# Routed attention with a squared-ReLU feed-forward: how the second pair of heads is turned, and how the first one is marked

## The chip, the cores and the metric

The kernel runs on one core of a Trainium2 chip. Its engines are TensorE (PE; its weight loads are PEld), VectorE (DVE), ScalarE (ACT), GpSimd (POOL) and SyncE (SP, which here only issues transfers). The metric is the device time of one execution in microseconds: 864.44 us before, the median of three runs (864.1 to 864.48).

## The reference

```python
# attention: q, k, v are (4, 8, 768, 64), centroids (8, 16, 64)
q_assign = np.argmax(np.einsum('bhsd,hcd->bhsc', q_n, c_n), axis=-1)   # normalised rows
k_assign = np.argmax(np.einsum('bhsd,hcd->bhsc', k_n, c_n), axis=-1)
mask = q_assign[:, :, :, None] == k_assign[:, :, None, :]
scores = np.where(mask, scale * np.matmul(q, k.transpose(0, 1, 3, 2)), -1000000000.0)
attn = softmax(scores)                     # over the keys
x = (attn @ v), brought to (3072, 512)
# feed-forward: w_in (512, 2048), w_out (2048, 512)
out = np.maximum(x @ w_in, 0.0) ** 2 @ w_out
```

A query thus attends to the keys of its own head that have the same nearest centroid.

## The kernel before

**Work.** The 32 heads are taken two at a time: 16 pairs, numbered from 0. One pass of the loop `for p in range(NG)` is the stage of pair p. A pair's q and k (768 rows of 64, two heads side by side in 128 partitions) are needed turned, with the 64 numbers of a row along the partitions: `qkT[p]`, 12 blocks of 128 columns, six of q and six of k. The scores are made in nine tiles, each two heads wide and 1024 columns in PSUM: tiles 0 to 5 hold a block of 128 keys against 512 queries, tiles 6 to 8 two blocks of keys against the other 256. For each tile TensorE runs `mask` (L456) and `score` (L447), ScalarE the exponential (L463) and VectorE the sums (L466). Then `times_v` (L481) multiplies all exponentials by v, `evict` (L490) copies the result, `add_up` (L500), `invert`, `spread` and `finish` divide by the sums. Three PSUM buffers (`ps_sc`, taken by `begin`) go round among the tiles, the logits and the add-up; two more banks, `V` and `M`, take the products with v. Beside the stages the weights of the feed-forward are loaded in blocks and rounded for later; after the last stage the feed-forward itself runs on TensorE to the end.

**Turning.** Pair 0 is turned on TensorE by multiplying with the identity (`turn_first`, L280). Pair 1 also (`turn`, L295: three calls of 16 matrix instructions each, copied to `qkT[1]` by ScalarE). From pair 2 on it is done by transfers: `split_words` (L315, L316) copies q or k on ScalarE into a tile `flat`, low and high halves of the 4-byte words apart, and writes it to DRAM as `words`; `turn_words` (L327) reads `words` back by one transposing transfer of 2-byte elements. `flat` has its place among the six buffers of q and k.

**Marks.** `logits` (L335) multiplies the turned rows by the normalised centroids; `turn_logits` (L346) brings the 16 logits of a row side by side; `number` finds the largest. Its steps are a maximum, a comparison `is_ge`, a product with 16, 15, ..., 1, a maximum again (so of equal maxima the first counts), and then for pair 0 an `is_equal` that gives a one-hot tile `oh`. `turn_onehot` turns it on TensorE (L402), and ScalarE and VectorE copy it out so that one matmul adds 0 where the clusters agree and a large negative number where not. For the other pairs `number` makes three rows of the number and its square (`marks`), which go to DRAM (`far`, L383) and back into `rows` (two transfers, L386) and do the same as three rows in place of sixteen.

**Order.** Each engine's instructions run in the order in which the program writes them, SyncE's transfers too. An instruction that waits holds up all behind it on its engine; a transfer issued from SyncE or ScalarE that must wait holds up that engine's queue. What SyncE issues in the first stages, in this order: q and k of pairs 0, 1, 2 and v of pair 0; then, at the top of stage 0,

```python
if p == 0:
    load_qk(3)
    load_ahead(0)          # weight blocks 0, 1, 2
...
load_v(p + 1)
```

and later in stage 0 `far` and `rows` of pair 1, `turn_words(2)`, the words of pair 3; in stage 1 `far_r` (`invert`, L515), `turn_words(3)`, two transfers of `spread` (L522), v of pair 2, `far` and `rows` of pair 2 (made by `number(2)` behind tile 3), the words of pair 4. `load_ahead(n)` loads weight blocks until n + 3 have been loaded. A block is rounded at the end of the stage of its number (`round_1`, ScalarE). In the later stages p the marks of pair p + 1 are made at the top of the stage.

At the end the sums' reciprocals, kept in `seen`, are examined: where one is not usable, a slower path computes all again (`check_sums`, L1707).

## Time and profile before

| | |
|---|---|
| median of three runs | 864.44 us |
| profiled execution | 866.05 us, its span 864.3 us |
| granted TensorE clock, mean | 0.999 |
| TensorE busy | 854.1 us, 99% of the span |
| VectorE / ScalarE / GpSimd busy | 86% / 52% / 28% |
| DMA | 174.36 MB, 202 GB/s in the mean |
| stage 0, from pair 0's logits to its first product with v | 10.35 to 27.00 us |
| stage 1, first mask to first product with v | 35.67 to 46.37 us |
| stage 2, first mask | 55.70 us |

A row of the timeline has start, length (both us), engine, line, operation, what is written from what, shape and count; idle time of the engine ahead of it and what ended it stand in brackets. SPq and ACTq are the issues of transfers: their length is that of the issue, not of the transfer. Ends of matmuls are modelled, so TensorE's waits show less as idle time than as later starts.

### The profile page before, as it was taken

The page shows a single profiled execution, that of the slowest core. Times are in us where ns is not written, and L with a number is a line of the kernel's source. Part 1 is how long each engine was busy: PE and PEld are TensorE (multiplying, and loading weights), DVE is VectorE, ACT ScalarE, POOL GpSimd, SP SyncE. Part 2 cuts the span into 40 slices and gives each one's busy share as a digit, 9 for nine tenths or more (in the row PEclk, how much of TensorE's full clock was granted, in tenths as well). Part 3 has the DMA queues.
Part 4 walks back from the last instruction along what each step waited for, and adds up shares of the span by engine and source line. Part 5 has one row for each costly group of instructions (what it writes and reads, how often), then busy time and mean ns, then how long its engine had stood idle before and what let it go on. Part 6 is the DMA issues. An engine that isn't in the chain of part 4 may idle for free.

```text
span 864.3 us, 15572 instructions
## 1 busy us (share of the span) xinstructions
PE 854.1 (99%) x5883; PEld 648.7 (75%) x5883; DVE 739.8 (86%) x1192; ACT 452.7 (52%) x697; POOL 245.9 (28%) x232
## 2 busy tenths in 40 slices
PE   9999999999999999999999999999999999999997
PEld 6444444444444445557899899999999999999997
DVE  5799888888888899899778888789888998888786
ACT  4877766677776557753212593122259322594120
POOL 0000001000000046772496537040233902337000
PEclk9999999999999999999999999999999999999999
DMA  7686797777766217829897634549447895444542
GB/s 257 152 202 177 208 283 197 191 195 189 192 173 162 83 45 246 255 76 323 328 334 267 233 135 143 211 136 338 173 174 235 285 372 200 170 146 135 222 151 74
DMA packets 149732, 174.36 MB, mean 202 GB/s; under 512 B 57258, under 2 KB 126994, under 8 KB 146322
## 3 DMA queue, kind: packets, MB, share of 16 engines
q1 hardware_dynamic: 133090, 152.94, 56.1%
q10 hardware_dynamic: 16560, 20.35, 7.2%
q8 instruction: 48, 0.79, 0.4%
q14 instruction: 34, 0.28, 0.1%
HBM read 111.98 MB, written 50.27 MB: 188 GB/s over the span
## 4 chain that ended last, share of the span: by engine, by line
PE 95%; DVE 2%; DMA 2%; ACT 0%; issue 0%; DVEq 0%
PE bank L1383 24%; PE bank L1111 16%; PE sc L447 14%; PE av_a L481 10%; PE bank L811 8%; PE bank L1280 6%; PE more L1111 5%; PE av_b L481 5%; PE sc L456 4%; PE sc L335 1%; PE sc L500 1%; DMA wt<-w_far 1%; DVE home L557 1%; DMA q_raw<-in_q_dram 0%; PE sc L280 0%; PE av_a L295 0%
## 5 line engine op out<-in xcount | busy, mean ns | idle before, releaser
L463 ACT ACTIVATE ex<-sc 128x1024 f32<-128x1024 f32 x144 | 144.4, 1026 | 37.5 <-PE sc L447 31.6
L447 PE MATMUL sc<-qkT 64*128 64x512 f32 (+1 forms) x768 | 150.5, 484 | 0.0
L167 POOL TENSOR_TENSOR w_in<-w_in,w_raw 128x512 int32<-128x512 int32 x16 | 21.4, 1340 | 296.4 <-DVE w_in L159 296.4
L1096 POOL TENSOR_TENSOR g<-g,home 128x384 f32<-128x384 f32 x60 | 61.0, 1048 | 156.0 <-DVE home L1195 101.7
L447 PEld LDWEIGHTS sc<-qkT 64*128 64x128 f32 x768 | 65.6, 188 | 42.1 <-issue 30.2
L481 PE MATMUL av_a<-ex,v_raw 128*64 128x512 f32 x384 | 85.9, 596 | 0.0
L466 DVE TENSOR_TENSOR total<-total,ex 128x1024 f32<-128x1024 f32 x64 | 78.7, 1229 | 6.5
L1640 ACT COPY spare<-bank 128x128 f32<-128x128 f32 x35 | 9.2, 263 | 133.2 <-issue 69.7
L1383 PE MATMUL bank<-wt,l 128*128 128x128 f32 x544 | 72.0, 275 | 0.2 <-DVE l L557 0.2
L1383 PE MATMUL bank<-wt,home 128*128 128x128 f32 x552 | 70.5, 275 | 0.0
L1383 PEld LDWEIGHTS bank<-wt,l 128*128 128x128 f32 x544 | 66.2, 192 | 0.4 <-DVE l L557 0.4
L1383 PEld LDWEIGHTS bank<-wt,home 128*128 128x128 f32 x552 | 66.0, 192 | 0.0
L1195 DVE TENSOR_TENSOR g<-bank,g 128x384 f32<-128x384 f32 (+2 forms) x108 | 53.2, 504 | 13.4 <-PE bank L1111 9.6
L481 PEld LDWEIGHTS av_a<-ex,v_raw 128*64 128x64 f32 x384 | 26.1, 137 | 51.0 <-issue 50.0
L1078 ACT COPY home<-bank 128x384 f32<-128x384 f32 x66 | 30.9, 480 | 58.2 <-PE bank L1111 56.8
L456 PE MATMUL sc<-rows 64*128 64x512 bf16 (+1 forms) x360 | 58.8, 323 | 0.0
L787 ACT ACTIVATE g<-g 128x768 f32<-128x768 f32 (+1 forms) x77 | 55.8, 725 | 2.4
L786 ACT ACTIVATE g<-g 128x768 f32<-128x768 f32 (+1 forms) x77 | 54.9, 713 | 2.9 <-DVE g L1195 1.5
L481 PE MATMUL av_b<-ex,v_raw 128*64 128x256 f32 x384 | 44.2, 379 | 0.0
L481 PEld LDWEIGHTS av_b<-ex,v_raw 128*64 128x64 f32 x384 | 27.6, 137 | 20.7 <-issue 5.7
L456 PEld LDWEIGHTS <-rows 64*128 64x128 bf16 x360 | 17.5, 94 | 33.6 <-issue 30.4
L1383 PE MATMUL bank<-wt,g 128*128 128x128 f32 x304 | 38.8, 275 | 0.0
(296 smaller groups left out, 1855.4 us busy)
## 6 DMA issues: line engine op xcount, KB each, us to landing
wt<-right_far SPq DMA_DIRECT2D x11, 1792.0 KB
wt<-w_far SPq DMA_DIRECT2D x20, 896.0 KB
words<-flat SPq DMA_DIRECT2D x26, 384.0 KB
w_raw<-in_moe_w_in_dram SPq DMA_DIRECT2D x16, 512.0 KB
w_raw<-in_moe_w_out_dram SPq DMA_DIRECT2D x16, 512.0 KB
wt<-right_far SPq DMA_DIRECT2D x7, 1024.0 KB
v_raw<-in_v_dram SPq DMA_DIRECT2D x16, 384.0 KB
raw<-raw_far SPq DMA_DIRECT2D x12, 512.0 KB
```

The lines of the kernel that those rows point to most:

```text
L447: nc.tensor.matmul(sc[i][:, e, cols], lhsT=qkT[pair][rows, NCH + c], rhs=qkT[pair][rows, n.start // P : n.stop // P], start=first, stop=no ...
L456: nc.tensor.matmul(sc[i][:, e, cols], lhsT=ohT[pair][rows, 1, c * P : (c + 1) * P], rhs=ohT[pair][rows, 0, columns(i)], start=first, stop= ...
L463: nc.scalar.activation(out=ex[i], in_=sc.pop(i), func=ACT.Exp, scale=SCALE)
L466: eng.tensor_tensor(out=out, in0=a, in1=b, op=ALU.add)
L481: nc.tensor.matmul(bank[D * e : D * (e + 1), 0 : n.stop - n.start], lhsT=raw_v[pair][:, e, c], rhs=ex[i][:, e, cols], start=c == 0, stop=c ...
L786: nc.scalar.activation(out=to, in_=to, func=ACT.Relu)
L787: nc.scalar.square(to, to)
L811: nc.tensor.matmul(bank, lhsT=operands[j][0][:, kk], rhs=operands[j][1][:, kk], start=(kk == 0), stop=(kk == H2 - 1),)
L1096: nc.gpsimd.tensor_tensor(out=of_four(to, s)[:, f, half], in0=of_four(base, s)[:, f, half], in1=beside[s][:, u], op=ALU.add,)
L1111: nc.tensor.matmul(bank[:, QT * u : QT * (u + 1)], lhsT=lefts[j, s](u)[i], rhs=operand[i], start=begins and u == 0, stop=True, skip_group_ ...
L1195: nc.vector.tensor_tensor(out=out, in0=one, in1=two, op=ALU.add)
L1383: nc.tensor.matmul(bank, lhsT=left[:, f], rhs=rhs[:, f], start=(f == 0), stop=(f == F4 - 1))
```

## The change

Pair 1 is now turned as the later pairs are. Behind pair 0's marks ScalarE splits its words (`split_words(1, i, nc.scalar)`), with `flat` in a buffer of the exponentials; SyncE issues `turn_words(1)` first in stage 0, in two transfers, q and k apart, each when its words have landed. `turn` and its copies go. `logits(1)` moves from behind tile 2 to ahead of tile 8 and writes to bank `M`; the last sum of tiles 0 to 5 comes behind pair 1's marks. `turn_words(2)` moves behind them too, and so does the load of pair 1's v. Of the weight blocks only block 0 is loaded in stage 0 (`load_ahead(-2)`); blocks 1 and 2 come in stage 1 by `load_ahead(0)`, behind v of pair 2. Pair 3's words keep their place.

Pair 0's one-hot tile is written by the `is_ge` itself, so that equal maxima give more than one mark. `count_marks` counts them: where a partition's marks are not 24 in number, the new last column of `seen` is not usable, and the slower path runs. The last quarter of pair 0's turned rows is copied by ScalarE and VectorE, half each (`by_two`). In stage 1 the scores of tiles 0 and 1 are made ahead of their masks.

```diff
--- before.py
+++ after.py
@@ -221,7 +221,7 @@
             scalar2=of_query, op0=ALU.mult, op1=ALU.add,
         )
 
-    seen = const.tile([P, NG * NBL], F32, name="seen")
+    seen = const.tile([P, NG * NBL + 1], F32, name="seen")
 
     oh = accp.tile([P, NBL, 2, D], BF16, name="oh", tag="part")
     nc.vector.memset(oh, 0.0)
@@ -286,22 +286,6 @@
         if which == 1 and i == 1:
             raw.pop(0)
 
-    def turn(pair, part, bank):
-        if part == 0:
-            qkT[pair] = qktp.tile([P, 2 * NCH, P], F32, name="qkT")
-        for i in range(4):
-            which, c = divmod(4 * part + i, NCH)
-            for e in range(2):
-                nc.tensor.matmul(
-                    bank[D * e : D * (e + 1), P * i : P * (i + 1)],
-                    lhsT=raw[pair][which][:, e, c], rhs=ident, start=True, stop=True,
-                )
-        nc.scalar.copy(
-            out=qkT[pair][:, 4 * part : 4 * part + 4].rearrange("p c n -> p (c n)"), in_=bank
-        )
-        if part == 2:
-            raw.pop(pair)
-
     words = {}
 
     def split_words(pair, which, queue=nc.sync):
@@ -309,7 +293,13 @@
             return
         if which == 0:
             words[pair] = dram.tile([2 * NCH, P, 2, 2 * D], U16, name="words")
-        flat = loads.tile([P, NCH, 2, 2 * D], U16, name="flat", tag="qk")
+        if pair == 1:
+            spare = expp.tile([P, 2, 512], F32, name="ex").bitcast(U16)
+            flat = spare.rearrange("p a n -> p (a n)")[:, 0 : 4 * S // 2].rearrange(
+                "p (c two d) -> p c two d", c=NCH, two=2
+            )
+        else:
+            flat = loads.tile([P, NCH, 2, 2 * D], U16, name="flat", tag="qk")
         src = raw[pair][which].bitcast(U16).rearrange("p h c (d two) -> p h c two d", two=2)
         for e in range(2):
             nc.scalar.copy(out=flat[:, :, :, D * e : D * (e + 1)], in_=src[:, e])
@@ -324,10 +314,13 @@
         if pair >= NG:
             return
         qkT[pair] = qktp.tile([P, 2 * NCH, P], F32, name="qkT")
-        nc.sync.dma_start(
-            qkT[pair].rearrange("p c n -> p (c n)").bitcast(U16),
-            words.pop(pair).rearrange("c p two d -> (c p two) d"), transpose=True,
-        )
+        far = words.pop(pair)
+        for i in range(0, 2 * NCH, NCH if pair == 1 else 2 * NCH):
+            c = slice(i, i + (NCH if pair == 1 else 2 * NCH))
+            nc.sync.dma_start(
+                qkT[pair][:, c].rearrange("p c n -> p (c n)").bitcast(U16),
+                far[c].rearrange("c p two d -> (c p two) d"), transpose=True,
+            )
 
     def logits(pair, bank):
         hp = pair % HP
@@ -355,17 +348,17 @@
             return t.unsqueeze(2).to_broadcast([P, n, C])
 
         nc.vector.reduce_max(out=mx, in_=src, axis=AX.X)
+        if pair == 0:
+            nc.vector.tensor_tensor(
+                out=oh.rearrange("p b e c -> p (b e) c")[:, :, 0:C], in0=src, in1=over_c(mx),
+                op=ALU.is_ge,
+            )
+            return
         nc.vector.tensor_tensor(out=best, in0=src, in1=over_c(mx), op=ALU.is_ge)
         nc.vector.tensor_tensor(
             out=best, in0=best, in1=order.unsqueeze(1).to_broadcast([P, n, C]), op=ALU.mult
         )
         nc.vector.reduce_max(out=mx, in_=best, axis=AX.X)
-        if pair == 0:
-            nc.vector.tensor_tensor(
-                out=oh.rearrange("p b e c -> p (b e) c")[:, :, 0:C], in0=best, in1=over_c(mx),
-                op=ALU.is_equal,
-            )
-            return
         squared = small.tile([P, n], F32, name="squared")
         nc.vector.tensor_tensor(out=squared, in0=mx, in1=mx, op=ALU.mult)
         for i, of in enumerate((squared, mx, squared)):
@@ -388,13 +381,23 @@
                 far[:, :, NBL * e : NBL * (e + 1)].rearrange("f g b i -> f g (b i)"),
             )
 
+    def count_marks():
+        marked = small.tile([P, 1], F32, name="marked")
+        nc.vector.reduce_sum(
+            out=marked, in_=oh.rearrange("p b e c -> p (b e) c")[:, :, 0:C], axis=AX.XY
+        )
+        nc.vector.tensor_scalar(
+            out=seen[:, NG * NBL :], in0=marked, scalar1=2.0 * NBL, scalar2=0.5,
+            op0=ALU.is_equal, op1=ALU.mult,
+        )
+
     def turn_onehot():
         spare = expp.tile([P, 2, 512], F32, name="ex").bitcast(BF16)
         ohT[0] = spare.rearrange("p a n -> p (a n)")[:, 0 : 2 * S].rearrange(
             "p (a n) -> p a n", a=2
         )
 
-        for half, bank in enumerate((sc.pop("oh")[:, 0], M)):
+        for half, bank in enumerate((V, M)):
             n = NBL // 2
             blocks = slice(n * half, n * (half + 1))
             po = bank.bitcast(BF16)[:, 0 : n * P].rearrange("p (b g i) -> p b g i", b=n, g=4)
@@ -606,18 +609,25 @@
             load_weights(loaded)
             loaded += 1
 
+    def by_two(out, in_):
+        nc.scalar.copy(out=out[:, 0:QT], in_=in_[:, 0:QT])
+        nc.vector.tensor_copy(out=out[:, QT:], in_=in_[:, QT:])
+
+    QT = TB // 2
     centroids_norm()
     turn_first(0, 0, V, nc.scalar.copy)
     turn_first(0, 1, M, nc.scalar.copy)
     halves = [ps_sc.tile([P, 2, 512], F32, name="sc")[:, 0] for _ in range(2)]
     turn_first(1, 0, halves[0], nc.scalar.copy)
     centroids_turned()
-    turn_first(1, 1, halves[1], nc.vector.tensor_copy)
+    turn_first(1, 1, halves[1], by_two)
     logits(0, begin("ls"))
-    for i in ("oh", 0, 1):
+    for i in range(2):
         begin(i)
     turn_logits(0)
     number(0)
+    for i in range(2):
+        split_words(1, i, nc.scalar)
 
     first_sums = []
     x_early, w_early = x_sums(FEED[0]), []
@@ -629,8 +639,9 @@
 
     for p in range(NG):
         if p == 0:
+            turn_words(1)
             load_qk(3)
-            load_ahead(0)
+            load_ahead(-2)
         if p == HP + 1:
             nc.sync.dma_start(x_far[FEED[3]], xT.pop(FEED[3]))
         if p:
@@ -642,25 +653,31 @@
         if 2 < p + 1 < NG:
             turn_logits(p + 1)
             number(p + 1)
-        load_v(p + 1)
         if p:
+            load_v(p + 1)
             load_ahead(p - 1)
 
 
         if p == 0:
             for i in range(2):
-                turn(1, i, (V, M)[i])
                 score(p, i, 0, True)
             turn_onehot()
+            count_marks()
             for t in rows_of:
                 nc.vector.memset(t, 0.0)
-            turn(1, 2, V)
+            begin(2)
+            score(p, 2, 0, True)
             for i in range(NB):
-                if i == 2:
-                    begin(i)
-                    score(p, i, 0, True)
                 mask(p, i, 0, False)
                 exponential(i)
+        elif p == 1:
+            for i in range(2):
+                begin(i)
+                score(p, i, 0, True)
+            for i in range(2):
+                mask(p, i, 0, False)
+                exponential(i)
+            tile_of(p, 2)
         else:
             for i in range(NB):
                 tile_of(p, i)
@@ -669,7 +686,6 @@
         add(nc.vector, first, ex[0], ex[1])
         if p == 1:
             tile_of(p, NB)
-        if p < 2:
             logits(p + 1, begin("ls"))
             turn_logits(p + 1)
             number(p + 1)
@@ -677,17 +693,25 @@
         for i in range(NB, NCH):
             if p != 1 or i > NB:
                 tile_of(p, i)
-            add(nc.vector, first, first, ex[i])
+            if p or i + 1 < NCH:
+                add(nc.vector, first, first, ex[i])
         if p == 0:
             for i in range(2):
                 split_words(2, i, nc.scalar)
-            turn_words(2)
         else:
             split_words(p + 3, 0)
 
 
         for i in range(NCH, NCH + NB):
             tile_of(p, i)
+            if p == 0 and i == NCH + 1:
+                sc["ls"] = M.rearrange("p (a n) -> p a n", a=1)
+                logits(1, sc["ls"])
+                turn_logits(1)
+                number(1)
+                turn_words(2)
+                load_v(1)
+                add(nc.vector, first, first, ex[NCH - 1])
         part = accp.tile([P, 2, 512], F32, name="part")
         add(nc.vector, part, ex[NCH], ex[NCH + 1])
         add(nc.vector, part, part, ex[NCH + 2])
@@ -1704,7 +1728,7 @@
         every = more.tile([1, 1], F32, name="every", tag="more")
         nc.tensor.matmul(every, lhsT=fine, rhs=ups[:, 0:1], start=True, stop=True)
         nc.vector.tensor_scalar(
-            out=flag[0:1], in0=every, scalar1=UP * float(P * NG * NBL), scalar2=None, op0=ALU.is_lt
+            out=flag[0:1], in0=every, scalar1=UP * float(P * (NG * NBL + 1)), scalar2=None, op0=ALU.is_lt
         )
 
     class Rounding:
```

## Rows read from the trace of the kernel before

**Rows 1.** The page's chain that ended last, shares of the span by engine.
```profile
PE 95%; DVE 2%; DMA 2%; ACT 0%; issue 0%; DVEq 0%
```

**Rows 2.** Timeline of TensorE in the stages of pairs 0 to 2.
```profile
19.50 0.85 PE L335 MATMUL sc<-qkT,cnT 128*32 128x384 f32 x8
...
27.00 5.37 PE L481 MATMUL av_a<-ex,v_raw 128*64 128x512 f32 x24
...
35.67 0.39 PE L456 MATMUL sc<-rows 64*128 64x512 bf16 x2
...
46.37 5.37 PE L481 MATMUL av_a<-ex,v_raw 128*64 128x512 f32 x24
...
55.70 0.39 PE L456 MATMUL sc<-rows 64*128 64x512 bf16 x2
```

**Rows 3.** Chain of waits, 10 to 28 us: start, length, what.
```profile
11.92 1.02 PE av_a L295 x16
12.94 1.06 PE sc L447 x4
...
16.86 1.05 PE av_a L295 x16
```

**Rows 4.** Timeline of VectorE, 10 to 22 us.
```profile
10.47 0.56 DVE L285 COPY qkT<-sc 128x384 f32<-128x384 f32 x1 [0.92 <-PE sc L280]
...
13.16 0.56 DVE L358 TENSOR_TENSOR best<-lt,mx 128x384 bf16<-128x384 f32 x1
...
14.94 0.56 DVE L364 TENSOR_TENSOR oh<-best,mx 128x384 bf16<-128x384 bf16 x1
...
21.54 0.57 DVE L346 STREAM_TRANSPOSE lt<-sc 128x384 f32<-128x384 f32 x1
```

**Rows 5.** Timeline of ScalarE, 16 to 30 us.
```profile
16.56 0.87 ACT L410 ACTIVATE ex<-sc 128x384 bf16<-128x384 bf16 x2 [0.90 <-PE sc L402]
...
18.42 2.86 ACT L463 ACTIVATE ex<-sc 128x1024 f32<-128x1024 f32 x3
...
24.77 1.55 ACT L315 COPY flat<-q_raw 128x768 uint16<-128x768 uint16 x2
...
28.88 1.03 ACT L463 ACTIVATE ex<-sc 128x1024 f32<-128x1024 f32 x1 [0.46 <-ACT flat L315]
```

**Rows 6.** Timeline of SyncE: issues of transfers.
```profile
10.88 1.41 SPq L128 DMA_DIRECT2D w_raw<-in_moe_w_in_dram  x3
...
25.76 0.38 SPq L383 DMA_DIRECT2D far<-marks_t  x1
28.60 1.68 SPq L386 DMA_DIRECT2D rows<-far  x2
31.34 5.14 SPq L327 DMA_TRANSPOSE qkT<-words  x1
...
41.60 3.71 SPq L327 DMA_TRANSPOSE qkT<-words  x1
...
46.64 1.55 SPq L105 DMA_DIRECT2D v_raw<-in_v_dram  x1
48.28 0.42 SPq L383 DMA_DIRECT2D far<-marks_t  x1
51.36 1.52 SPq L386 DMA_DIRECT2D rows<-far  x2
...
77.07 3.25 SPq L327 DMA_TRANSPOSE qkT<-words  x1
```

**Rows 7.** DMA rate in 40 slices: 10:21, 31:42, 41:52 and 76:87 us.
```profile
GB/s 380 374 369 240 89 128 168 279 397 406 402 268 223 253 209 149 179 238 253 343 283 358 358 402 343 432 402 361 380 378 309 207 194 115 91 54 39 28 22 11
...
GB/s 84 112 357 419 296 73 101 221 139 174 172 111 151 182 195 323 323 276 189 176 304 238 10 7 37 290 289 290 315 348 350 344 343 350 346 350 259 0 0 0
...
GB/s 136 0 0 0 0 0 23 216 183 27 122 106 182 165 269 285 292 289 292 288 250 61 190 279 346 268 134 56 78 128 212 352 374 315 145 166 195 296 374 313
...
GB/s 22 20 28 2 0 0 0 0 56 243 85 59 171 289 291 289 290 290 290 290 239 90 268 302 302 235 231 99 24 2 0 5 0 0 0 0 145 190 290 363
```

## The prediction

> **What bounds the kernel now.** I read the page first, then the chain of waits over the first 28 us, then the timelines of VectorE, ScalarE, TensorE and SyncE's queue, and last the DMA rate in fine slices. TensorE is busy for 99% of the span (the table above) and is 95% of the chain that ended last [rows 1]: time is won only by taking work or waits out of TensorE's order, and whatever makes TensorE wait costs its full length. Everything that the change touches lies in the stages of pairs 0 and 1 (before 56 us). From the stage of pair 2 on the order is the old one, so I reduce the question to one event: when does the first mask matmul of pair 2 start? Before it is at 55.70 [rows 2]; I add its shift to the time. The sum is made against the profiled execution (866.05 us, span 864.3), which is 1.61 above the median 864.44; a forecast for the median is the sum less 1.61.
>
> **Turning pair 1 on TensorE (removed).** Three batches of 16 instructions stand in the chain at 1.02 to 1.05 us each, from the one at 11.92 to the one at 16.86 [rows 3]: 3.09 us. A score behind a turn costs 1.06 there; behind a score I take 0.86, an estimate: the 1.09 of a tile (below) less 0.23 for its mask. So 0.2 comes back once.
>
> **First marks by the maxima alone.** Of VectorE's steps after the logits, the `is_ge` at 13.16 now writes the one-hot tile, and three steps up to the one at 14.94 go [rows 4], 0.56 each with gaps: one-hot ready at 13.5 in place of 15.5. This is needed, not gained: without the turns TensorE has only two scores (1.06 + 0.86) between the logits and the one-hot transposes and would otherwise wait. The count (a reduction like the 0.56 one, and a small step) stands behind the one-hot copies on VectorE, ahead of two memsets and of the first sum, which waits for exponentials: nothing. The extra column of `seen`: nothing. Copying the last turned half on two engines halves the 0.56 us copy at 10.47 [rows 4], for which the logits wait: it is over at 10.83 in place of 11.03, and the logits, whose end at 11.92 is where the first turn starts in the chain [rows 3], end at 11.72: 0.2 gained.
>
> **Splitting pair 1 on ScalarE (added).** The same four copies and two DMA issues for pair 2 take from 24.77 to the next exponential at 28.88: 4.11 us [rows 5]. Pair 1's q and k were long there (TensorE turned them from 11.85 without a wait), so the copies start at 10.85, behind ScalarE's half of the turned tile, and hold ScalarE till 14.96; the one-hot copies behind them (0.87, [rows 5]) end at 15.85. TensorE gets there by 11.72 (logits) + 1.92 (two scores) + 0.77 (one-hot: what is left to 16.86 of the chain behind two turns and two scores from 11.92) + 1.06 (third score) = 15.47, so it waits 0.4. The exponentials then run from about 16.5 and not 18.42 [rows 5], and they set the pace: three score buffers, so tile 3 waits for exponential 0 (17.5), where TensorE has been done at 16.6: 0.9 lost. A tile takes 1.09: pair 1's nine tiles and one group of logits (0.85) lie between 35.67 and 46.37 [rows 2]. Six tiles from 17.5 and pair 1's logits, now ahead of tile 8, bring the products with v to 24.8 or 24.9, against 27.00 [rows 2]: 2.2 gained of the 3.3 removed.
>
> **Pair 1's transposing transfers.** The key words are issued at 14.5, 0.4 before ScalarE is free again. Pair 2's went out as long before the exponential at 28.88 [rows 5] and let SyncE's queue go on at 31.34 [rows 6], so 2.9 later: landed at 17.4. A transposing transfer of a whole pair on a quiet queue (issued at 77.07) has its traffic over by 81.8 [rows 6, 7]; half of one some 3.5 us: 20.9. Bounds: 2 us, and the 7.4 that pair 2's took beside other loads [rows 6, 7]. The logits of pair 1 come at 22.9 (one tile and their own 0.85 ahead of 24.8): I take no wait. Queued behind on SyncE are pair 3's loads and one weight load; both were used behind the exponentials at 28.88, and are there in time by 5 us and more.
>
> **Pair 1's marks.** VectorE began to read pair 1's logits at 21.54 [rows 4], and `far`, the marks' way out, went at 25.76 [rows 6]: 4.22 us. It begins now at 23.75, so `far` goes at 28.0, and by the 2.84 from `far` to the row transfers and their 1.68 [rows 6] these are issued by 32.5. Pair 1's tiles now begin with two bare scores: the products and the add-up took 8.67 us before (27.00 to 35.67, [rows 2]), so the scores start at 33.5 and the first mask at 35.4. That is behind the rows' landing by any of the bounds below, so no wait. I take 0.2 us for the changed order and 0.3 for waits on exponentials, which start later in the stage: pair 1's products begin at 33.5 + 10.7 + 0.5 = 44.7 against 46.37 [rows 2], and 9.33 later (46.37 to 55.70) pair 2's first mask would come by TensorE's own order, at 54.0: 1.7 us gained.
>
> **What SyncE's queue makes of it.** It runs in written order. Pair 2's transposing transfer was issued at 31.34, now at 32.5 behind the later rows; v of pair 1 now follows it (0.39 MB, 1.1 us at the 350 GB/s of [rows 7]). Before, pair 3's words ran undisturbed for 2.5 us (38.7 to 41.2, [rows 7]) and the next transposing transfer was released at 41.60 [rows 6]. In place of a transfer that ran 7.4 us beside a load from ScalarE's queue (that load is now over before) I take the quiet 4.7: 32.5 + 4.7 + 1.1 + 2.5 + 0.4 = 41.2. So far even.
>
> But behind it, ahead of pair 2's `far`, now stand two weight loads that the old kernel had issued with a third at 10.88 [rows 6]: `load_ahead(-2)` leaves them to the stage of pair 1. Before, v at 46.64 and `far` at 48.28 follow each other; v's traffic ends at about 50.4, and the rows can be issued at 51.36, when `far` has landed [rows 6, 7]. `far` landed only after v's traffic, as if it stood behind it. Two loads of 0.524 MB each cost 2.8 us at the 370 GB/s that [rows 7] reach and 4.1 at 255, the mean over the forty slices of the stretch in which such loads ran before. I take 3.2, nearer the low end, since the old loads ended in a tail that nothing followed. Then: v over at 50.0, weights at 53.2, `far` landed (0.95 later, as before) at 54.15, the rows' two issues 1.5 (1.52 in [rows 6]) and their landing 1.0 (bounds: 0.7, a small transfer with no delay, and 2.8, the latest that leaves no wait at 55.70): the mask at 56.65. TensorE, there at 54.0, waits 2.65. **Sum: 56.65 - 55.70 = +0.95 us, 867.0 for the profiled execution, 865.4 for the median.**
>
> The Trainium skill, *DMA: Bandwidth & Descriptors*, section "Queues, rings and completion order", says that on each DMA engine a queue's descriptors are taken in ring order. By that rule `far` can't pass the weight loads, and the forecast stands; were small transfers let through, the time would be that of the first rival below. The trace agrees: `far`, issued at 48.28, landed some 0.95 us after v's traffic ended and not before it.
>
> **Rivals.** (1) *Not late.* `far` passes the weights, or these fill gaps in the traffic (61 and 56 GB/s slices stand in [rows 7]), and pair 2's mask starts at 54.0 or at best 53.0, if the waits on ScalarE cost less: -1.7 to -2.7, 861.7 to 862.7. For it: the old stretch from 41 to 52 us has many slices under 200 GB/s [rows 7], so there is room; against: that room lies mostly ahead of the transposing transfer's traffic, where the weights are not yet issued. (2) *Slower: pair 2's transposing transfer is starved again.* Place: the queue from 32.5. Price: 7.4 in place of 4.7, and all behind it is 2.7 later: +3.65, 868.1. It decides once the transfer takes over about 5.5 us, from which the sum is beyond +1.73. For it: the old transfer in this place ran with breaks, down to 10 and 7 GB/s [rows 7]; against: the load that it shared the engines with has moved away. (3) *Slower: pair 1's turned halves come after 22.9*, since the first transposing transfer of the old kernel was its slowest (5.14 us of issue, 3.25 at 77.07 [rows 6]). At 7.4 for the second half it lands at 24.8 + 0.4: 2.3 us of wait, which `far`, rows and queue all inherit: +3.2, 867.7.
>
> **How the numbers follow.** Forecast (late by the weights): 0.62, from +0.3 (weights 2.8, rows' landing 0.7, queue 0.3 the earlier for it) to +2.8 (weights 4.1, landing 2.0), 864.7 to 867.2. Not late: 0.15. Starved: 0.14. Pair 1 late: 0.09. A measurement of this kernel tells about 0.2% (1.73 us) from no change, so same is 862.7 to 866.2. Faster is 0.13, all of the first rival but its edge; same is 0.02 from there, 0.48 of the forecast and 0.03 of mild forms of the others, 0.53; slower is the forecast's upper end, 0.14, with 0.20 of the two slow rivals: 0.34. The range takes half of each side: 862.4 to 867.8.
>
> **What would show it.** Right: no L295 turns and the products with v of pair 0 starting at 24 to 25.5; a wait of TensorE of 2 to 3.5 us ahead of pair 2's first mask (L456 `rows`), and on SyncE a wait of 4 us or more between pair 2's `far` and its rows, with two `w_raw` issues ahead of them; from there to the end the old span within 0.3 us. Wrong: no wait there (rival 1), a logits wait for a transposing transfer near 23 us (rival 3) or near 38 (rival 2), or a gain or loss that arises after 60 us, for which I see no cause.

## The result, and the profile after

The changed kernel takes 871.92 us in the median (16 runs, 867.05 to 879.19) against 864.11 for the kernel before in the same session (16 runs, 861.78 to 866.38): ratio 1.0106, interval [1.0086, 1.0127]. It is slower, and above the range of the forecast. The profiled execution takes 872.58 us (span 870.7), 6.5 more than the one before. Medians and ratios leave out executions that took far longer than all others of their kernel (one of e15 below, at 2294.76 us, and three of the kernel before).

The executions of the changed kernel differ by 12.1 us, those of the kernel before by 4.6. The mean granted clock goes with it: 0.997 in the fastest of the changed kernel, 0.989 in the slowest. The profiled one has 0.995 and 8.4 us at half the clock; the slowest must have some 19 (an estimate: 2.2 times the shortfall), at places that no trace shows. What follows is the account of one execution, near the median.

TensorE after, timeline of the stages of pairs 0 to 2, to be read against [rows 2]:

```profile
20.53 0.85 PE L328 MATMUL av_b<-qkT,cnT 128*32 128x384 f32 x8
...
22.50 5.37 PE L484 MATMUL av_a<-ex,v_raw 128*64 128x512 f32 x24
...
33.00 0.81 PE L459 MATMUL sc<-rows 64*128 64x512 bf16 x6
...
37.60 0.85 PE L328 MATMUL sc<-qkT,cnT 128*32 128x384 f32 x8 [1.86 <-DMA qkT<-words]
...
55.97 0.39 PE L459 MATMUL sc<-rows 64*128 64x512 bf16 x1 [2.69 <-DMA rows<-far]
56.74 0.61 PE L459 MATMUL sc<-rows 64*128 64x512 bf16 x1 [0.38 <-DMA rows<-far]
56.75 2.31 PE L450 MATMUL sc<-qkT 64*128 64x512 f32 x4
```

The products with v of pair 0 start 4.5 us earlier, pair 2's logits (before at 40.08) 2.5 earlier, behind a wait for the transposing transfer, and pair 2's first masks 0.3 and 1.0 later, behind a wait for the row transfers. SyncE's issues, the answer to [rows 6]:

```profile
25.68 0.37 SPq L376 DMA_DIRECT2D far<-marks_t  x1
27.35 1.67 SPq L379 DMA_DIRECT2D rows<-far  x2
29.14 4.91 SPq L320 DMA_TRANSPOSE qkT<-words  x1
...
40.85 2.69 SPq L320 DMA_TRANSPOSE qkT<-words  x1
...
44.89 0.54 SPq L105 DMA_DIRECT2D v_raw<-in_v_dram  x1
45.48 0.94 SPq L128 DMA_DIRECT2D w_raw<-in_moe_w_in_dram  x2
46.47 0.43 SPq L376 DMA_DIRECT2D far<-marks_t  x1
53.71 1.52 SPq L379 DMA_DIRECT2D rows<-far  x2
```

`far` goes 1.8 us earlier than before and its rows 2.35 later: 7.2 us between them in place of 3.1, with two weight loads ahead of `far`. What follows is in the table by stretches (from:to, length, then busy time and instructions of PE, PEld, DVE, ACT, POOL, granted clock, DMA share, GB/s), of the kernel after:

```profile
56.70:60.10 3.40, 3.35 (x10) 2.18 (x12) 2.01 (x7) 1.00 (x1) 0.00 (x0) 0.50 0.67 200
...
606.30:609.70 3.40, 3.40 (x13) 3.40 (x12) 0.00 (x0) 1.16 (x3) 0.00 (x0) 0.50 0.98 324
```

and of the kernel before:

```profile
56.70:60.10 3.40, 3.40 (x22) 1.50 (x20) 3.22 (x7) 3.00 (x3) 1.22 (x1) 1.00 0.32 67
...
606.30:609.70 3.40, 3.40 (x23) 3.40 (x22) 1.95 (x5) 0.96 (x2) 0.00 (x0) 1.00 0.90 296
```

Twice TensorE stood still and then got the lower level (0.50, 1.2 GHz) for 3.4 us: in the same 3.4 us it did 10 matmuls in place of 22, and 13 in place of 23. Its largest waits after (line, tile, releaser: sum, times, longest):

```profile
PE sc L459 <- DMA rows<-far: 3.1, 2, 2.7
PE bank L1135 <- DMA raw<-raw_far: 2.3, 1, 2.3
PE sc L328 <- DMA qkT<-words: 1.9, 1, 1.9
...
PE bank L1135 <- DVE spare L560: 0.7, 1, 0.7
```

Aligning the two traces matmul by matmul, the kernel after is 2.5 us ahead at pair 2's logits, 1.0 behind at pair 2's second mask, 2.7 behind at 60 us (the half clock), 1.25 at 507 us, and 6.4 behind from 610 us to the end. (The fall of about a microsecond near 492 us belongs to the trace of before: e4 below, the old kernel with a wider tile, gains 0.9 there too.) So there are two losses: one in stages 1 and 2, foretold, with a half clock behind it that wasn't; and one of 5.2 us near 600 us, in the feed-forward part, whose order of instructions the change leaves alone.

The second in rows. ScalarE's and SyncE's issues near 587 us before:

```profile
584.96 2.23 ACTq L1591 DMA_DIRECT2D out_dram<-g  x4
...
587.32 0.81 SPq L968 DMA_DIRECT2D wt<-w_far  x2
588.35 1.18 SPq L1771 DMA_DIRECT2D xT<-x_far  x2
592.16 0.32 SPq L937 DMA_DIRECT2D raw<-raw_far  x1
```

and after:

```profile
586.19 2.88 ACTq L1615 DMA_DIRECT2D out_dram<-g  x4
...
586.71 0.81 SPq L992 DMA_DIRECT2D wt<-w_far  x2
589.53 7.56 SPq L1795 DMA_DIRECT2D xT<-x_far  x2
598.16 0.32 SPq L961 DMA_DIRECT2D raw<-raw_far  x1
```

Before, the two weight loads go when all four stores `out_dram<-g` are issued; after, they go between the first store and the last, the second `xT` load waits 6.9 us for a store, and `raw` is issued 6.0 us later. What the DMA view has of instruction loads (queue 8), before in 583:584 us, and after in 587:588, is one each:

```profile
q8 instruction: 1, 0.02, 5.5%
```

These are loads of 16,384 bytes, 48 over the span; they are TensorE's code: with 160 recorded TensorE instructions more (e6 below) there are 49, and the places of the loads move with the count. The page counts 5883 matmul records and as many weight loads before, 5835 of each after: the removed turns are 96 recorded instructions, so each code load falls at another place of the same work.

### The profile page after: what moved, and what is told of

It reads as the page before. It is cut to its first block, busy times and chain, and to the rows that moved or that the text cites. A ratio compares the mean times of both kernels' runs of the same rounds, so it can differ in the third digit from the quotient of the medians.

```text
span 870.7 us, 15481 instructions
## 1 busy us (share of the span) xinstructions
PE 853.2 (98%) x5835; PEld 649.2 (75%) x5835; DVE 740.4 (85%) x1191; ACT 453.2 (52%) x699; POOL 245.6 (28%) x232
## 3 DMA queue, kind: packets, MB, share of 16 engines
q1 hardware_dynamic: 136226, 153.73, 56.6%
## 4 chain that ended last, share of the span: by engine, by line
PE 87%; DVE 8%; DMA 3%; issue 1%; ACT 0%; SPq 0%; DVEq 0%; ACTq 0%
PE bank L1407 22%; PE bank L1135 16%; PE sc L450 14%; PE av_a L484 9%; PE bank L835 8%; PE more L1135 5%; PE av_b L484 4%; PE bank L1304 4%; PE sc L459 3%; PE sc L328 1%; DMA far<-marks_t 1%; PE sc L503 1%; DMA qkT<-words 1%; DVE spare L1219 1%; DVE x_t L560 1%
## 5 line engine op out<-in xcount | busy, mean ns | idle before, releaser
L450 PE MATMUL sc<-qkT 64*128 64x512 f32 (+1 forms) x768 | 152.5, 488 | 0.0
L450 PEld LDWEIGHTS sc<-qkT 64*128 64x128 f32 x768 | 67.8, 189 | 41.9 <-issue 30.8
L459 PE MATMUL sc<-rows 64*128 64x512 bf16 (+1 forms) x360 | 60.8, 325 | 3.1 <-DMA rows<-far 3.1
```

The source lines that it names most:

```text
L450: nc.tensor.matmul(sc[i][:, e, cols], lhsT=qkT[pair][rows, NCH + c], rhs=qkT[pair][rows, n.start // P : n.stop // P], start=first, stop=no ...
L459: nc.tensor.matmul(sc[i][:, e, cols], lhsT=ohT[pair][rows, 1, c * P : (c + 1) * P], rhs=ohT[pair][rows, 0, columns(i)], start=first, stop= ...
```

## The experiments

Each was timed in five rounds beside the kernel before. "Shift" is how much later than in the profile of before the same matmul starts. The upper clock begins at 3.9 us (e8) to 10.0 (before), as it happens, and that alone moves what follows: pair 0's products start at 22.50 in after, at 24.38 in e15, where it begins 3.4 us later. So shifts of two traces compare only to about 2 us, while a step within one trace is sharper.

**Where weight blocks 1 and 2 stand (e1, e2, e3) and the tile layout (e4).** e1 is the kernel after, with the loads back in stage 0:

```diff
-            load_ahead(-2)
+            load_ahead(0)
```

> The changed kernel with weight blocks 1 and 2 loaded in stage 0 again, behind pair 3's q and k. Queue theory (the two weight loads ahead of pair 2's `far` make TensorE wait about 3 us before pair 2's first mask, and the halved clock that follows costs 1.7 more): the mask comes at 53 to 54 us in place of 56.7, the clock stays at its upper level from the ramp to the end, and the time falls by 4 to 9 us to 861 to 867. Layout theory (the extra column of `seen` moves the buffers allocated behind it and slows transfers near 600 us): it stays at 868 to 873, with the wait for `raw` near 604 us. Turning theory (the transposing transfers of pair 1 themselves cost it, by the 1.9 us wait of pair 2's logits): the wait at 36 to 38 us stays, the time falls by 1 to 2 us at most.

870.63 us, 1.0070 [1.0042, 1.0097]. In stage 0 the three loads delay pair 1's `far` and rows (rows issued at 31.62 in place of 27.35) and with them all of stage 1; pair 2's second mask comes at 56.84, not at 53 to 54. Near 603 us TensorE waits 2.7 us, with half the clock behind it. The old place cost nothing in the old order alone.

e2 puts them between `far` and the rows of pair 2:

```diff
+        if pair == 2:
+            load_ahead(0)
         rows = ohT[pair] = rows_of[pair % 2]
...
-            load_ahead(p - 1)
+            if p > 1:
+                load_ahead(p - 1)
```

> The changed kernel with weight blocks 1 and 2 issued in stage 1 between pair 2's `far` and its `rows`. Queue theory: `far` lands some 3 us earlier, the mask at 53 to 55.5 (the rows now share the engines with the weights), little or no fall of the clock, 862 to 867. Layout theory and turning theory as for the other: 868 to 873, or 1 to 2 us less than that.

870.53 us, 1.0068 [1.0043, 1.0094]. The rows are issued earlier (51.55) but stand behind the weights in the queue: TensorE waits 3.5 us for them, and the clock is half from 57.5 to 60.9. The loss near 600 stays.

e3 is the kernel before with the loads moved late, and nothing else:

```diff
-            load_ahead(0)
+            load_ahead(-2)
```

> The kernel before with nothing changed but weight blocks 1 and 2 loaded in stage 1, behind v of pair 2 and ahead of its `far`. Queue theory: `far` lands 2.5 to 3.5 us later than 51.36, pair 2's mask waits 0.8 to 2 us; 865 to 867, with a halved clock behind the wait up to 868. Layout and turning theories: 864, no difference.

868.88 us, 1.0058 [1.0037, 1.0078]. This alone makes the old kernel wait, in TensorE's list of waits:

```profile
PE sc L456 <- DMA rows<-far: 2.6, 2, 2.3
```

the first mask of pair 2 comes at 58.54 in place of 55.70, the clock is half from 60.5 to 63.9, and the shift behind it is 5.2, at the end 4.3. Near 600 us nothing happens. So the moved loads alone make the first loss.

e4 is the kernel before with `seen` one column wider, which moves what is placed behind it in memory:

```diff
-    seen = const.tile([P, NG * NBL], F32, name="seen")
+    seen = const.tile([P, NG * NBL + 1], F32, name="seen")
```

> The kernel before with `seen` one column wider (the column is never written or read). Layout theory: slower by 3 us or more, with waits for transfers near 600 us. Queue and turning theories: 864, no difference that can be told.

864.79 us, 1.0008 [0.9995, 1.0022]: the layout theory is out.

**Code loading, both ways (e5, e6, e9).** e5 is the kernel after with TensorE's 96 recorded instructions put back as 24 small matmuls; e6 is the kernel before with 160 more (`range(40 * p)`), which is 256 less 96. The edit shown is e5's:

```diff
-            logits(p + 1, begin("ls"))
+            bank = begin("ls")
+            for _ in range(24):
+                nc.tensor.matmul(bank[:, 0, 0:1], lhsT=ident, rhs=ident[:, 0:1], start=True, stop=True)
+            logits(p + 1, bank)
```

> The kernel after, with 24 more matmuls of one column (written into the bank that logits(2) overwrites, just before it). Theory (code loading): the change took 24 f32 matmuls, which are 96 recorded TensorE instructions, out of the first pair, so every 16 KB load of TensorE's code (queue 8 in the DMA view) falls at another place of the same work; near 584 us of the kernel before such a load holds up the transfers xT<-x_far and out_dram<-g on one DMA engine by 2 us, near 587 us of the kernel after it holds up out_dram<-g instead, which SyncE's second xT<-x_far waits for (6.9 us). With the 96 instructions back the load falls where it fell before: SyncE's wait near 590 is under 1 us, TensorE's wait for raw<-raw_far (2.3 us) and the half clock near 607 are gone, and the time is 3 to 4.5 us under the kernel after (867.5 to 869), less up to 2 us that the 24 matmuls may cost where logits(2) does not wait. Rival (the four more DMAs shift which semaphore each DMA counts on, or chance): the wait near 590 stays at about 7 us and the time at 871 to 873. The stage 2 wait for rows<-far (2.7 us) stays by both.

> The kernel before, with 40 more matmuls of one column just before logits(2) (160 recorded TensorE instructions; 160 more and 96 fewer differ by 256, which is one 16 KB load of 64-byte instructions). Theory (code loading): the loads fall at the same places of the FFN's work as in the kernel after, and SyncE's second xT<-x_far near 590 waits some 7 us for out_dram<-g, TensorE some 2 us for raw<-raw_far, with half the clock behind it: 864 + 2 (the 40 matmuls) + 3.5 = 868 to 870.5. Rival (semaphores, or chance): no such wait, 864 to 866.5.

e5: 871.83 us, 1.0077 [1.0048, 1.0105]; e6: 881.17 us, 1.0180 [1.0151, 1.0209]. By the traces the theory holds both ways. In e5 no wait for `raw` is left and SyncE's `xT` waits 0.3 us; its shift is 4.3 from 50 us on and 3.4 at the end, with no step near 600. In e6, the old program with its old transfers, SyncE and TensorE have the waits of the kernel after. Waits of SyncE's queue, 575 to 612 us, and of TensorE, whole span:

```profile
SPq L1774 <- DMA out_dram<-g: 8.3, 2, 6.4
```

```profile
PE bank L1114 <- DMA raw<-raw_far: 1.2, 1, 1.2
...
PE bank L1114 <- DMA home<-raw_far: 0.8, 1, 0.8
```

and the shift grows by 3.0 us between 507 and 617 us. The rival falls: e5 keeps the four additional DMAs, and e6 has none. The totals missed, since the small matmuls cost far more than I allowed. In e6, TensorE's timeline and a stretch of the table by windows:

```profile
39.51 14.15 PE L675 MATMUL sc<-ident 128*128 128x1 f32 x80
```

```profile
42.90:56.50 13.60, 13.60 (x66) 11.68 (x67) 1.27 (x3) 0.00 (x0) 0.00 (x0) 0.50 0.45 108
```

TensorE was busy without a break, and yet the granted clock fell to 0.50 from 42.9 to 56.6 us (in e5 from 42.6 to 46.0). e9 repeats e5 with matmuls of the removed form:

```diff
+                nc.tensor.matmul(bank[0:D, 0, 0:P], lhsT=ident[:, 0:D], rhs=ident, start=True, stop=True)
```

> The kernel after, with 24 f32 matmuls of 64 weight columns and 128 columns (the form that the change removed, 96 recorded TensorE instructions) just before logits(2), in place of the 24 one-column ones, behind which the clock fell to half for 3.4 us and which took 5.67 us. Theory (code loading, and full columns keep the clock): some 3.3 us at the upper clock (16 of them took 1.09 us in the kernel before) of which 1.9 lie in the wait for qkT<-words; no half clock before 50 us; no wait for raw<-raw_far near 604. Shift at 60 us as in after (+2.7) or up to 1.5 less where the lateness of TensorE covers the wait for rows, and the same shift at the end: 867 to 869.5. Rival (code loading costs nothing of its own): 871 to 873.

868.82 us, 1.0042 [1.0024, 1.0060]: 3.1 us under the kernel after, and 0.64% in the ratio, though the 24 matmuls took 5.45 us, not 3.3. No half clock within the kernel, no wait for `raw`, and the shift goes from 4.8 at 60 us to 3.9 at the end. Over all traces the step near 600 us is 4.9 to 5.2 us where half the clock follows it (after, e1, e2, e15), 2.9 to 3.2 where it does not (e6, e7, e10, e14), and 0.3 at most with the old count of TensorE instructions (e3, e4, e5, e8, e9, e11). So the place of the code loads is worth 3 to 5 us.

**The other places for the loads (e7, e8, e10, e11, e12, e14).** In e7 both weights follow pair 2's rows; in e8 v of pair 2 does too, with e5's 24 small matmuls (the edit is e8's; e7 lacks the `load_v(2)`, and both leave out the old place):

```diff
                 far[:, :, NBL * e : NBL * (e + 1)].rearrange("f g b i -> f g (b i)"),
             )
+        if pair == 2:
+            load_v(2)
+            load_ahead(0)
```

> The kernel after, with weight blocks 1 and 2 issued behind the two rows(2) transfers of the third pair instead of ahead of far(2). Theory (SyncE's queue): far(2) near 47, rows(2) near 51 and nothing ahead of them, so TensorE's first mask of the third pair comes at 53.7 to 54.5 instead of 55.97, with a wait under 0.6 us and the clock kept behind it; the gain over the kernel after is 1.5 + 1.7 (the half clock) = 2.5 to 4 us at 60 us, 868 to 869.5 in all, as the wait near 590 us stays. Rival (the wait is the transposing transfers' or far's own): rows(2) still issue after 53 and the wait is over 2 us, 871 to 873.

> The kernel after, with v of the third pair and weight blocks 1 and 2 behind the rows(2) transfers, and the 24 matmuls of one column of the run above it. Theory: both losses go, rows(2) issue still earlier (49 to 51 us), and what is left is the gain of stage 0: 861.5 to 864, at or up to 2.5 us under the kernel before. Rival: if the losses are of another cause, 868 to 872.

e7: 872.32 us, 1.0076 [1.0051, 1.0102]. The first mask of pair 2 did come at 54.88 with a wait of 0.5, but then ScalarE stood still for a weight (its waits):

```profile
ACT w_in L139 <- DMA w_raw<-in_moe_w_in_dram: 10.6, 1, 10.6
```

TensorE waited 3.6 us for exponentials behind it, and the clock fell at 63.2. So the loads have a deadline on the other side as well. e8: 871.62 us, 1.0078 [1.0052, 1.0104]; the small matmuls took 7.85 us, with half the clock from 38.1 to 48.3, which hides the rest. Its trace shows that with no load ahead `far` needs 2.2 us (48.82 to 51.03), and no wait for `raw` is left. Next, both weights at the end of stage 0 and v behind the rows (e10; e11 with e9's matmuls), or the weights behind pair 3's transposing transfer (e14; e12 with 12 matmuls, below):

```diff
                 load_v(1)
+                load_ahead(0)
...
             turn_words(p + 2)
+            if p == 1:
+                load_ahead(0)
```

(the first edit is e10's, the second e14's.)

> The kernel after, with weight blocks 1 and 2 issued at the end of stage 0 (behind v of the second pair, ahead of the words of the fourth) and v of the third pair behind rows(2). Theory (SyncE's queue between two deadlines: early loads delay far and rows, late ones stop ScalarE, which waited 10.6 us for w_raw when they stood behind rows(2)): far(2) has nothing ahead of it, rows(2) issue at 49 to 52 us, the first mask of the third pair comes at 54 to 54.8 with a wait under 0.5 us, ScalarE does not wait for w_raw over 1 us, no half clock at 57 to 64; shift at 65 us against before -1.7 to 0; then the loss near 600 as in after (+3.5): 865 to 868. Rival (turn(3) then comes late: the fourth pair's words wait behind the weights): TensorE waits for qkT<-words at logits(3), 1 to 3 us, 868 to 871.

> Both edits of the two runs above together. Theory: neither the wait for rows nor the one near 600 is left; what is left of the gain of stage 0 shows: 862 to 865, the same as before or up to 2 us faster. Rival: 866 to 871.

> The kernel after, with weight blocks 1 and 2 issued in stage 1 right behind turn_words(3) (ahead of rb and far(2)) and v of the third pair behind rows(2). Theory (SyncE's queue): turn(3) keeps its place (41 to 43 us), far(2) at 46 to 48 us lands behind the two blocks at about 49, rows(2) issue at 49 to 51 us, the first mask of the third pair does not wait over 0.6 us (53.7 to 55 us by the start of the upper clock), ScalarE waits under 2 us for w_raw, no half clock at 55 to 65; the shift against before at 65 us is -2 to 0. Near 600 us the wait for raw<-raw_far stays as in after: 865.5 to 868.5. Rival (it is not these loads that delay rows): rows(2) issue after 53, 870 to 873.

> Both edits of the two runs above together. Theory: neither the wait for rows nor the one near 600, what is left is the gain of stage 0 less the wait for qkT<-words: 862 to 865, between 2 us faster than before and the same. Rival: 866 to 871.

e10: 870.87 us, 1.0071 [1.0047, 1.0096]; e11: 869.45, 1.0047 [1.0029, 1.0065]. The rival's mechanism holds: pair 3's words wait behind the weights, and its transposing transfer goes at 47.9 and 47.6 in place of 40.85. But the wait that it foretold, at pair 3's logits, does not come; pair 2's rows are late instead, at 56.3 and 56.4, and TensorE waits up to 1.7 and 1.6 us for them. e14: 872.21, 1.0103 [1.0086, 1.0120]; e12: 869.08, 1.0063 [1.0042, 1.0084]. The transposing transfer keeps its place, but behind two loads `far` takes 5.8 and 5.1 us, and TensorE waits 4.3 and 3.9: I had allowed 2 us. In all four theory fell short, by size or by the rival's mechanism.

**Half of the instructions (e13).** The kernel after with 12 matmuls that write the two halves of a bank in turn:

```diff
+            for i in range(12):
+                half = slice(D * (i % 2), D * (i % 2 + 1))
+                nc.tensor.matmul(
+                    bank[half, 0, P * (i // 2 % 4) : P * (i // 2 % 4 + 1)], lhsT=ident[:, half],
+                    rhs=ident, start=True, stop=True,
+                )
```

> The kernel after, with 12 f32 matmuls of 64 weight columns and 128 columns before logits(2), half of the 24 of the run that had 96 recorded instructions more; they write the two halves of a bank in turn, as the removed ones did (16 recorded ones took 1.09 us). Theory (code loading): 48 recorded instructions bring the 16 KB load that falls at 587.4 us in the kernel after some 3 to 4 us earlier, between 581 and 586 us, where it holds up out_dram<-g(1) and with it wt<-w_far until the four out_dram<-g are issued: no wait for raw<-raw_far near 604; the matmuls cost 1.6 us of TensorE inside the wait for qkT<-words (1.9): 866 to 869. Rival (it takes the exact place of before): the wait stays, 870 to 873.

870.42 us, 1.0078 [1.0059, 1.0096]. The matmuls took 1.53 us and fill the wait for the transposing transfer; no wait for `raw` is left, 1.0 us for `home`, and SyncE's `xT` waits 3.6 us in place of 6.9. But my reason was off. Counted from the issue of `right_far`, which opens this exchange of transfers, the code load comes at 4.5 us in the traces of before, e3, e4, e5, e8, e9 and e11, at 7.1 to 7.2 after and in e1, e2, e6, e7, e10, e14 and e15, and at 6.9 to 7.0 here and in e12 and e16, not 3 us earlier; the weight loads still go between the stores.

The semaphore events of the traces show what these tenths decide. Each of these transfers counts sixteen completions on a semaphore. The second `xT` load counts on the same one as the `out_dram<-g` store issued some 6.5 us behind `right_far`, in all eighteen traces, and in the eleven where the code load comes late it is issued 0.06 to 0.07 us after the last of the store's sixteen. That store is complete 3.1 to 3.3 us after its issue in the first group. In the second group twelve or more completions come within 6.0 us, and one to four are late, the last at 9.5 to 10.2 us: after, fifteen come in time and the last at 10.1. In the third group the last comes at 6.8 (e13) and 5.4 to 5.5 us (e12, e16), and the step near 600 us is 1.5, 0.5 and 0.6. So a few late completions of one store carry the difference; why a load of code 0.2 us later makes them so late isn't shown. The store and the load that share a semaphore are the same two before and after, so the rival of shifted semaphores falls by this too.

**Both causes at once (e15, e16).** e15 gives each load the place its deadline asks for: weight 1, which ScalarE rounds in stage 1, at the end of stage 0, and weight 2 and v behind the rows. e16 adds e13's 12 matmuls:

```diff
                 load_v(1)
+                load_ahead(-1)
...
+        if pair == 2:
+            load_v(2)
+            load_ahead(0)
```

> The kernel after, with weight block 1 issued at the end of stage 0 behind v of the second pair, and v of the third pair and weight block 2 behind rows(2): the one block that ScalarE rounds at the end of stage 1 comes early, everything else stands behind rows(2). Theory (SyncE's queue between two deadlines): far(2) at 46 to 48.5 us with no load ahead of it, rows(2) 2 to 4 us later (2.2 where v and both blocks stood behind them), the first mask of the third pair waits under 0.6 us, ScalarE waits under 1 us for w_raw, no half clock at 55 to 65; shift against before at 65 us -2 to 0 by the start of the upper clock; then the loss near 600 as in after (some +3): 865 to 868. Rival (the wait comes from the copies of the second queue or the transposing transfer, not the loads on SyncE's): rows(2) still 5 us and more behind far(2), 870 to 873.

> The run above and 12 f32 matmuls before logits(2) as in e12 and e13 (there the matmuls took 1.53 us inside the wait for qkT<-words, and no wait for raw<-raw_far was left, 0.3 to 1.0 us for home<-raw_far). Theory: both causes are gone, 862.5 to 866, about the kernel before. Rival: 867 to 871.

e15: 867.40 us, 1.0043 [1.0024, 1.0062]. Its profiled execution waits four times for rows, 0.8 at most, keeps the clock up to 606 us, and has the second loss near 600 us, as TensorE's waits show:

```profile
PE bank L1140 <- DMA raw<-raw_far: 2.2, 1, 2.2
PE sc L462 <- DMA rows<-far: 1.9, 4, 0.8
PE sc L328 <- DMA qkT<-words: 1.9, 1, 1.9
```

This is the slowest of eleven executions, 872.63 us; six took 865.3 to 867.4, and whether they have the second loss isn't shown.

e16: 866.24 us, 1.0023 [1.0010, 1.0036], just above what was expected, with the upper clock from 8.6 us to 861.9; TensorE's waits for transfers:

```profile
PE sc L462 <- DMA rows<-far: 1.8, 3, 0.9
...
PE bank L1147 <- DMA home<-raw_far: 0.4, 1, 0.4
```

So the two causes hold most of the loss: of 1.06%, 0.6 goes with the places of the loads and 0.2 with 12 matmuls that compute nothing. The 0.2 is not clear of noise, as the two intervals overlap; between e14 and e12 the same matmuls are worth 0.4, which is. No version beat the kernel before: what stage 0 gains is eaten by the wait for pair 2's transposing transfer (1.9 us in e15; in e16 the 12 matmuls fill it) and by waits for rows, 1.8 us in three places.

## Why the prediction was wrong

*Stage 0, right.* Products with v were foretold at 24.8; they start at 22.50 with the upper clock from 5.5 us, and at 24.38 and 24.51 in e15 and e9, where it came at 8.9 and 9.4. Before it came at 10.0. So some 2.5 us are the change's, near the forecast's 2.2, and the other 2 are luck of the clock. Pair 1's halves were in time, by 0.2 us (landed at 20.31, used at 20.53): rival 3 did not happen.

*Pair 2's transposing transfer, mis-sized.* I took the quiet 4.7 us for it. It was issued at 29.14 and complete at 37.47, 8.3 us later. (Even the quiet one, issued at 77.07, was complete only 5.45 us later: I had read the end of its traffic.) Before it was complete 8.0 us after its issue, 0.7 ahead of TensorE's need; so an earlier issue alone could not bring the logits forward by more. Rival 2's starvation happened, though the load beside it was over; its price was smaller, 1.86 us of TensorE. That pair 3's transfer still went at 40.85 (41.2 foretold) is luck: pair 2's went 3.4 us earlier than foretold and took 3.6 longer.

*Pair 2's `far` behind two weights, right.* Foretold: `far` to rows over 4 us, a wait of 2 to 3.5, the mask at 56.65. Measured: 7.2 us (2.2 in e8, with no load ahead), waits of 2.69 and 0.38, masks at 55.97 and 56.74. The rows' landing, taken as 1.0 us behind their two issues, was 0.7 and 1.5. e3 shows the cause by itself; in e15, without it, no wait for rows is over 0.8 us.

*The sum ends there, wrong.* "From the stage of pair 2 on the order is the old one, so I reduce the question to one event" and "from there to the end the old span within 0.3 us" are the steps that failed, in two ways. A wait of that length was followed by 3.4 us at half the clock, 1.7 us that stood in no term (e3: 3.5 of shift became 5.2). And "a gain or loss that arises after 60 us, for which I see no cause" came to 5.2 us: the same order of instructions isn't the same run, since 96 fewer TensorE instructions move every later load of code, and one of these decides near 587 us which transfers go first and how late the last completion of a store comes (e5, e6, e9, e13). (The lower edge of the forecast, +0.3, does not come out of its own terms, 0.95 less 0.4, 0.3 and 0.3; nothing hangs on it, as the result lies on the other side.)

In the trace of before, of the sixteen completions of the `xT` load issued at 579.40 fifteen come within 5.0 to 5.4 us and one at 7.0, across the code load at 583.5; the store issued at 579.46 has the same late one, and `wt` waits for that store (issued 7.9 us behind it; after, where all sixteen come within 5.4 to 5.8, 6.0 us). The late completion held the weights back until the four stores were out. That happy order is not the whole mechanism: e12, e13 and e16 have the other order and most of the cure, as the last completion of the store ahead of the second `xT` load is less late there.

The Trainium skill, *Runtime: NRT & Kernel Launch*, section "Instruction fetch mechanics", says that code comes in 16 KiB blocks of 256 instructions by DMA and that crossing a block is mostly hidden. The trace agrees on the size (11,766 records and 48 loads, 245 for each) and no wait of TensorE for code stands in its list of waits; but hidden from the engine isn't hidden from the transfers beside it, and here the measurement says 3 to 5 us.

## What to carry to other kernels

When instructions are removed early on, expect every later code load of that engine to move, and check the transfers near the tightest waits, also in a part that the change does not touch. A load moved in a queue has a deadline on both sides: price what stands behind it in the new place, and who waits for it if it comes later. Add to every new wait of TensorE of some 2 us or more the stretch at half the clock that the traces show behind such waits.

## What the runs showed of the hardware

Matmuls of one column were no cheaper here than those of 128. In e9, 48 recorded passes of 128 columns into one place took 5.45 us at the upper clock (TensorE's timeline, as in the next fence):

```profile
37.68 5.45 PE L691 MATMUL sc<-ident 128*64 128x128 f32 x48
```

e5's 48 one-column passes took 5.67, partly at half the clock, and e13's 24 passes into alternate halves of a bank:

```profile
35.22 1.53 PE L692 MATMUL sc<-ident 128*64 128x128 f32 x24
```

114 ns a pass against 64. (e13's also alternate between two halves of the weights and four places in the bank; which of these counts isn't shown.) Where the clock fell within the profiled kernels, it was behind waits of TensorE of 1.7 us and more in all, or amid the one-column matmuls; not each such wait brought a fall (1.86 at 37.60 after did not). A DMA's issue can also wait for an older transfer with which it shares nothing but the semaphore. ScalarE stood idle 6.4 to 6.6 us in e12 to e14, ahead of its own load of k. The list of waits names `far<-marks_t`, but in e13 that landed at 55.12, and the load went at 52.88. It went 0.08 us after the last transfer on its own semaphore was complete: `rb` in e12 and e14 (53.58, 52.74), a weight in e13 (52.80).
